# Reordering the last pass of a two-layer decode backward kernel: streamed chunks ahead of kept ones

## The chip, the cores and the metric

The kernel runs on one core of a Trainium2 chip. The metric is the device time of one launch in microseconds (us). A core has TensorE (PE, matrix multiplies), VectorE (DVE), ScalarE (ACT), GpSimd (POOL) and SyncE (SP); in this kernel SP only issues loads and POOL mostly issues stores. Both kinds of transfer run on the same 16 DMA engines.

## What is computed

The reference is a forward pass of two layers, used twice, and its vector-Jacobian product (`jax.vjp`). Shortened:

```
def A(x, k_cache, v_cache, wq, wo):      # B=2, one query, 32 heads, 4 kv heads, Sk=16384, Dh=128
    q = (x @ wq) per head;  k, v = caches repeated 8 times
    p = softmax(q k^T / sqrt(Dh));  return (p v) @ wo
def B(x, w1, b1, w2, b2):                # D=1024, F=3584
    return gelu(layernorm(x) @ w1 + b1) @ w2 + b2
x = x + A(layernorm(x)); x = x + B(layernorm(x))
x = x + A(layernorm(x)); x = x + B(layernorm(x))
outputs: x, and the gradients of x, k_cache, v_cache, wq, wo, w1, b1, w2, b2
```

Everything is bf16. Each cache is 32 MiB, so each of dK and dV is 32 MiB to store; the weight gradients are another 30 MiB.

## The kernel before, in words

The caches are cut into 8 groups `g` (batch times kv head) of 4 chunks (`NCH`) of 1 MiB each, 32 chunks (`NC`) per cache. A chunk is a tile of 128 partitions by 8 KB, one contiguous 8 KB run of memory per partition. The forward layers and the backward of the upper layer read the caches chunk by chunk. The last pass is the backward of the lower attention layer, and it also makes everything that is stored: dK and dV (the sum over both layers), dwq, dwo, dw1, dw2.

**The last pass** begins at line 1396 and has its main loop at L1438. Chunk indices `i` follow `order`: the first group's four chunks (i = 0 to 3) are *kept*, that is they still lie in tiles `keepV0..3` and `keepK0..3` from earlier; the 28 others are *streamed* (loaded again; chunk 4 of both caches was kept too, in `keepxV`, `keepxK`). A step `m` of the loop does, in this order: for two slots `k`, eight transposes of a V chunk and their copy out (`kT`, L1453), the score products of the slot before last (`score0`, L1317) and, at the end of a chunk, `ds0` (L1319), which makes dX, the score gradient, on DVE; a turn of one dwq operand (`late_pe`); one half of a *pair* each for K (k = 0) and V (k = 1); then the operand block of the next pairs (`make_blks`, four transposes per cache, L999); what `Sched` has due (`dq_quad`, which multiplies dX with the K chunk into dq); some units of weight gradients (`step_fill`); and new loads (`pump`).

**A pair** (`kv_pair`, L1247) is what makes a 1 MiB chunk of dK or dV, in two halves `h`: each has eight matmuls into four PSUM banks and four copies of 128x512 into half of a *home* tile, and stores that half (512 KB, 4 KB per partition). `v_at` and `k_at` (L1432) say in which step a chunk's first half comes. Before: V chunk i in step 2i - 3 (from i = 2), K chunk i one step after 2i - 4 for a streamed chunk, and after i - 1 for a kept one (K 31 one step sooner). So the kept K chunks take steps 0 to 3 and the two kept V chunks that are left steps 1 and 3; V 0 and 1 are made ahead of the loop.

**Fill.** A unit (`dw_units`, L1162) is one matmul of 4 rows into 128x512 and one copy; 4 or 8 units fill a part of a home tile, which is stored as two rows of 128 at a time. There are 240 such units, two for the biases, and nine units (`rows_unit`) that turn operands into rows. Before, `step_fill` takes one in each of steps 0 to 3 and five in every later step. The last 16 units (the last quarter of dwq) can only be made when dq of the last group is known.

**Tiles.** Loads, homes and fill share about 16 tiles of 1 MiB. A tile that has been read goes on the list `by_read`, one whose store has been issued on `by_store`; homes come from `by_read` first, loads from `by_store` first, oldest first. A load into a tile whose store has not landed waits on the SP queue, and the loads behind it with it; a copy into such a home waits on its engine. `pump` keeps at most 10 loads open in the first four steps and 7 later. The tile of `keepV0` holds dX of the kept chunks until the block of K chunk 3 is made.

**The end.** After the last chunk's dX: two `dq_quad`, the copy of the sums (`evac`), `reduce`, then `quarter` (L1293), which puts the 16 last units on `late` and three items on `tail`: the products with wq in two parts (L1282) and the layer norm backward (`last`); then the store of the x gradient.

Of the kernel before, what the change touches and what calls it, by code (L numbers as in the profile page):

```python
# [9 lines left out]
BF16 = mybir.dt.bfloat16  # L10
# [13 lines left out]
def kernel(  # L24
# [25 lines left out]
    V = nc.vector  # L50
# [15 lines left out]
    TC = 32  # L66
    NCH = T // TC
# [959 lines left out]
            V.tensor_copy(out=diag[:, t], in_=gcols.unsqueeze(1).to_broadcast([128, 4, n]))  # L1027

    def q_make(w, g, bank):
        Qm = wrk2.tile([128, 2, 128], BF16, name="Qm" + w)  # L1030
        for t in range(2):
            PE.matmul(bank[:, t * 128:(t + 1) * 128], lhsT=spr[w][:, t * 128:(t + 1) * 128], rhs=ident[:],
                      start=True, stop=True)
        evac_cast(Qm[:].rearrange("p a b -> p (a b)"), bank[:, 0:256], 256)
        qms[w, g] = Qm
# [101 lines left out]
    def store(out_ap, view, tile_):  # L1137
        nc.gpsimd.dma_start(out_ap, view)
        if tile_ is not None:
            by_store.append(tile_)  # L1140
# [21 lines left out]
    def dw_units(xrows, yrows, i, chunks, y0, ny, out_of):  # L1162

        ps_, tpos = (slice(0, 128), None) if i is None else (slice(32 * i, 32 * i + 4), (32 * i, 0))
        box = {}
        units = []
        for j0, rb in chunks:
            for j in range(rb):
                for c0 in range(0, ny, 512):
                    def u(j0=j0, rb=rb, j=j, c0=c0):  # L1170
                        if j == 0 and c0 == 0:
                            box["t"] = new_home()
                        sv_ = box["t"][:, 0:rb * ny].rearrange("p (j n) -> p j n", j=rb)
                        ps = mx()
                        PE.matmul(ps[:], lhsT=xrows[ps_, (j0 + j) * 128:(j0 + j + 1) * 128],  # L1175
                                  rhs=yrows[ps_, y0 + c0:y0 + c0 + 512], start=True, stop=True, tile_position=tpos)
                        evac_cast(sv_[:, j, c0:c0 + 512], ps[:], 512)
                        if c0 + 512 >= ny and (j % 2 == 1 or j == rb - 1):
                            js = j - j % 2
                            store(out_of(j0 + js, j + 1 - js), sv_[:, js:j + 1], box["t"] if j == rb - 1 else None)  # L1180
                    units.append(Unit(u, j == 0 and c0 == 0))
        return units

# [61 lines left out]
    stgs = {}  # L1245

    def kv_pair(w, i, h):  # L1247

        g, c = chunks[i]
        if h == 0:  # L1250
            stgs[w, i] = new_home()
        sv_ = stgs[w, i][:].rearrange("p (b r t d) -> p b r t d", r=4, t=2, d=128)
        blk, Qm = blks[w, i], qms[w, g]
        o = 0 if w == "V" else NB
        pss = [mx() for _ in range(4)]
        for b in range(2):
            for r in range(4):
                PE.matmul(pss[r][:, b * 256:(b + 1) * 256], lhsT=blk[32 * r:32 * r + 32, o + 2 * h + b, :],  # L1258
                          rhs=Qm[32 * r:32 * r + 32, :, :].rearrange("p a b -> p (a b)"), start=True, stop=True,
                          tile_position=(32 * r, 0))  # L1260
        for r in range(4):
            evac_cast(sv_[:, 2 * h:2 * h + 2, r], pss[r][:].rearrange("p (b t d) -> p b t d", b=2, t=2), 512)
        dst = (dVv if w == "V" else dKv)[g, :, c * TC + h * TC // 2:c * TC + (h + 1) * TC // 2, :]
        store(dst, stgs[w, i][:, h * LDW // 2:(h + 1) * LDW // 2].rearrange("p (t d) -> p t d", d=128),
              stgs[w, i] if h == 1 else None)

    dwq_v = out_4.rearrange("(j p) n -> p j n", p=128)
    quarters = {}
# [7 lines left out]
    def in_rows(q, kv):  # L1276
        box, ps = q[4], pm_([128, 512], F32, "dn_tail")

        def part(a):
            for j in range(a, a + 4):  # L1280
                for o in range(8):
                    PE.matmul(wide_out(ps, 2 * j), lhsT=box[j - j % 4][:, j % 4, o * 128:(o + 1) * 128],  # L1282
                              rhs=wide_in(dq_all[:, kv * 8 + o, 0:2]), start=(o == 0), stop=(o == 7))

        def last():
            V.tensor_tensor(out=dn0[:], in0=dn0[:], in1=pairs(ps, DJ), op=ALU.add)
            g0 = attn_in_bwd(0, g1, dn0, lambda: step_fill(1), lambda: step_fill(2))
            tail.append(lambda: col_to_row_f32(g0, DJ, out_1.rearrange("b s d -> (b s) d"), "o1",
                                               ktp.tile([128, 8, 128], BF16, name="o1", tag="kT")))

        return [lambda: part(0), lambda: part(4), last]

    def quarter(kv):  # L1293

# [45 lines left out]
    def dq_quad(i, q):  # L1340
        g, c = chunks[i]
        accs[g].coef = lambda u: dX[i][:, u - c * CP, 0].rearrange("p h t -> p (h t)")
        accs[g].quad(c, q)
        if q == 1:
            if g == G - 1:
                by_read.append(held_tiles["K%d" % c])
            else:
                done("K", g, c)

    def score0(s):  # L1350
        i, b = NCH + s // NB, s % NB
        g, c = chunks[i]
        if b == 0:
            dps["t"] = pm_([128, 16, TC], F32, "dp")
        scores(i, b, kTs.pop(s), dps["t"])
        if b < NB - 1:
            return
        if c == 0:
            open_dq(g)
        if order.index(g) % 2 == 1 and c == (2 if i < 2 * NCH else 0):  # L1360
            quarter_loads(g % HKV)
        ds0(i, dps["t"][:])
        end = 1 if i == NC - 1 else 2
        sch.later(1, lambda: dq_quad(i, 0))
        sch.later(end, lambda: dq_quad(i, 1))
        if c == NCH - 1:
            sch.later(end, accs[g].evac)
            sch.later(end + 1, accs[g].reduce)

    def step_fill(n):  # L1370
        for k in range(n):
            for q in ((late, fill) if k % 2 == 0 else (fill, late)):
                if q and q[0].ready():
                    q.popleft()()
                    break
# [53 lines left out]

    v_at = {2 * i - 3: i for i in range(2, NC)}  # L1432
    k_at = {(i - 1 if i < NCH else 2 * i - NCH - (i == NC - 1)): i for i in range(NC)}
    make_blks(None, 0)
    NS = (NC - NCH) * NB
    zero = {}
    m = 0
    while 2 * m < NS + 12 or late or fill or late_pe or tail or m <= max(v_at) + 2:  # L1438
        sch.s = m
        qs = []  # L1440
        iv, ik = v_at.get(m + 1), k_at.get(m)
        for w, i in (("V", iv), ("K", ik)):
            if i is not None and chunks[i][1] == 0 and (w, chunks[i][0]) not in qms:
                qs.append(make_qm(w, chunks[i][0]))
        for k in range(2):
            s = 2 * m + k
            if s < NS:
                i, b = NCH + s // NB, s % NB
                cv = get("V", *chunks[i])[:].rearrange("p (t d) -> p t d", d=128)
                kT = ktp.tile([128, 8, 128], BF16, name="kT", tag="kT")  # L1450
                tp = mtp()
                for j in range(8):
                    PE.transpose(tp[:, j, :], cv[:, b * 8 + j, :], ident[:])  # L1453
                evac_bf16(kT[:].rearrange("p a b -> p (a b)"), tp[:].rearrange("p a b -> p (a b)"), 1024)
                kTs[s] = kT
                if b == NB - 1:
                    done("V", *chunks[i])
                if b == 0 and chunks[i][1] == 0:
                    wg = chunks[i][0]
                    V.tensor_copy(out=wide_do[wg][:, :, 3], in_=cols["V"][:, wg].rearrange("p l r -> p (l r)"))  # L1460
            if 0 <= s - 2 < NS:
                score0(s - 2)
            if late_pe and (k == 1 or s >= NS or len(late_pe) > 6):
                late_pe.popleft()()
            at, w, m_ = ((k_at, "K", m - 1), (v_at, "V", m))[k]
            for h in range(2):
                if at.get(m_ - h) is not None:
                    kv_pair(w, at[m_ - h], h)
            if tail:
                tail.popleft()()  # L1470
        for f in qs:
            f()
        if iv is not None or ik is not None:
            make_blks(iv, ik)
        sch.run_slot(1)
        if m == NS // 2 - 8:
            zero["t"] = new_home()
            nc.gpsimd.memset(zero["t"][:, 0:2 * D], 0.0)
            nc.gpsimd.tensor_copy(out=zero["t"][96:100, 0:D], in_=rowsB[96:100, :])
        step_fill(1 if m < NCH else 5)  # L1480
        pump(NLD + 3 if m < NCH else NLD, 3)
        m += 1

# [29 lines left out]
```

## Time and profile before

| what | us |
|---|---|
| median of 7 runs | 1143.64 (1140.7 to 1147.08) |
| the profiled execution | 1142.9 |
| its span, first to last instruction | 1141.1 |
| PE busy | 938.1 (82%) |
| DVE busy | 633.0 (55%) |
| ACT busy | 564.8 (49%) |
| POOL busy | 117.8 (10%) |
| first kT transposes of step 0 of the last pass | at 743.13 |
| those of step 9 | at 797.11 |
| those of step 49 | at 1055.32 |
| those of step 50 | at 1073.31 |
| dX of the last chunk (step 56) | at 1104.63 |

The profile has a page with busy times, the span in 40 slices, DMA queues (q1 carries the loads of SP, q0 the stores of POOL), the chain that ended last, and groups of instructions. Further views are tables by stage, the timeline of an engine or a queue, and waits. The DMA share of a stage is the mean busy share of the 16 DMA engines (it can read a little over 1), GB/s is what they moved.

### The profile page before, as it was taken

The numbers are of one execution on the slowest core, as the hardware profiler recorded it, in microseconds if no ns is written. First come the engines' busy times: TensorE is split into PE (matmuls) and PEld (weight loads), VectorE is DVE, ScalarE is ACT, GpSimd is POOL, SyncE is SP. The second block draws the span as 40 slices with busy tenths as digits, with TensorE's granted clock in tenths as the row PEclk, the third lists the DMA queues.
The fourth block names the chain that finished last, engine by engine and source line by source line (L and its number), as shares of the span: only waits on it lengthen the run. The fifth ranks groups of instructions, "written<-read, shape, count | busy, mean of one in ns | idle before, by whom it ended". The sixth has DMA issues, their size and how long they took to land. (4 is left out here: it accounts for less than half of the span.)

```text
span 1141.1 us, 40256 instructions
## 1 busy us (share of the span) xinstructions
PE 938.1 (82%) x17565; PEld 725.4 (64%) x17567; DVE 633.0 (55%) x1357; ACT 564.8 (49%) x1415; POOL 117.8 (10%) x206
## 2 busy tenths in 40 slices
PE   4988896487879885899997799989888888998585
PEld 3867674387767765888775588855555554554352
DVE  1535442133544433544845355678887876887385
ACT  0534351022535430344554354667777866867373
POOL 0000000000000000000000000022232222222323
PEclk9989785587998976899998799998988987987796
DMA  9999999998999989999999999998999999999997
GB/s 370 424 424 424 425 424 413 409 362 352 423 426 420 425 327 423 402 360 406 375 421 420 348 368 356 346 376 307 415 421 420 419 415 413 371 407 409 411 400 293
DMA packets 98717, 449.33 MB, mean 394 GB/s; under 512 B 8418, under 2 KB 8418, under 8 KB 67564
## 3 DMA queue, kind: packets, MB, share of 16 engines
q1 hardware_dynamic: 72204, 348.17, 76.1%
q0 software_dynamic: 26336, 98.60, 21.3%
q8 instruction: 137, 2.24, 0.7%
q14 instruction: 40, 0.33, 0.1%
HBM read 348.14 MB, written 98.58 MB: 391 GB/s over the span
## 5 line engine op out<-in xcount | busy, mean ns | idle before, releaser
L153 ACT COPY kT<-tp 128x512 int32<-128x512 int32 x209 | 122.8, 588 | 253.9 <-PE tp L420 243.0
L156 DVE COPY kT<-tp 128x1024 bf16<-128x1024 bf16 x159 | 108.7, 691 | 108.7 <-PE tp L420 96.9
L420 PE MATMUL tp<-ident,kv_K 128*128 128x128 bf16 x1728 | 142.9, 231 | 4.3 <-DMA kv_K<-in_A_k_cache_dram 4.0
L420 PEld LDWEIGHTS <-kv_K 128*128 128x128 bf16 x1728 | 108.6, 103 | 5.2 <-DMA kv_K<-in_A_k_cache_dram 4.5
L164 DVE CAST big<-xm 128x512 bf16<-128x512 f32 (+1 forms) x125 | 81.1, 685 | 36.3 <-DMA out_dram<-big 16.3
L161 ACT CAST big<-xm 128x512 bf16<-128x512 f32 (+1 forms) x139 | 75.7, 593 | 38.9 <-DMA out_dram<-big 17.6
L573 PEld LDWEIGHTS <-kT 128*128 128x128 bf16 x2048 | 76.3, 98 | 27.4 <-issue 21.2
L573 PE MATMUL sc<-qT_bf,kT 128*128 128x8 bf16 x2048 | 92.0, 171 | 0.2
L420 PE MATMUL tp<-ident,kv_V 128*128 128x128 bf16 x864 | 69.3, 226 | 11.6 <-DMA kv_V<-in_A_v_cache_dram 10.7
L270 PE MATMUL wtp<-ident,wt 128*128 128x128 bf16 x928 | 75.3, 228 | 3.8 <-issue 2.6
L537 ACT ACTIVATE e_all<-sc,negm 128x64 bf16<-128x64 f32 x256 | 77.2, 345 | 1.2 <-DVE negm L532 1.1
L306 PEld LDWEIGHTS <-wt 128*128 128x128 bf16 x1696 | 49.1, 104 | 43.9 <-issue 15.4
L161 ACT CAST keepV<-xm 128x512 bf16<-128x512 f32 x118 | 64.6, 595 | 23.0 <-PE xm L1258 17.2
L452 PE MATMUL acc_all<-kv_V,e_all 128*16 128x256 bf16 x864 | 46.2, 294 | 26.8 <-DMA kv_V<-in_A_v_cache_dram 13.9
L156 DVE COPY wT<-wtp 128x1024 bf16<-128x1024 bf16 (+1 forms) x64 | 40.7, 641 | 49.2 <-PE wtp L270 45.6
L153 ACT COPY wT<-wtp 128x512 int32<-128x512 int32 (+1 forms) x60 | 34.3, 572 | 64.1 <-PE wtp L270 49.9
L164 DVE CAST keepV<-xm 128x512 bf16<-128x512 f32 x86 | 55.7, 685 | 18.0 <-PE xm L1258 7.1
L164 DVE CAST keepK<-xm 128x512 bf16<-128x512 f32 (+1 forms) x87 | 56.5, 685 | 13.8 <-PE xm L1258 6.8
L420 PEld LDWEIGHTS <-kv_V 128*128 128x128 bf16 x864 | 54.7, 101 | 13.5 <-DMA kv_V<-in_A_v_cache_dram 11.4
L161 ACT CAST keepK<-xm 128x512 bf16<-128x512 f32 (+1 forms) x95 | 51.7, 592 | 19.3 <-PE xm L1258 12.0
L270 PEld LDWEIGHTS <-wt 128*128 128x128 bf16 x928 | 57.8, 102 | 4.5 <-issue 3.1
L537 ACT ACTIVATION_READ_ACCUMULATOR e_all<-sc,negm 128x1 f32 x256 | 60.1, 235 | 0.0
(368 smaller groups left out, 1823.8 us busy)
## 6 DMA issues: line engine op xcount, KB each, us to landing
kv_K<-in_A_k_cache_dram SPq DMA_DIRECT2D x81, 1024.0 KB, 12.2
kv_V<-in_A_v_cache_dram SPq DMA_DIRECT2D x81, 1024.0 KB, 12.1
wt<-in_A_wo_dram SPq DMA_DIRECT2D x32, 1024.0 KB, 10.9
out_dram<-big POOLq DMA_DIRECT2D x62, 512.0 KB, 15.6
wt<-in_B_w_dram SPq DMA_DIRECT2D x32, 896.0 KB, 14.1
out_dram<-keepV POOLq DMA_DIRECT2D x44, 512.0 KB, 14.1
out_dram<-keepK POOLq DMA_DIRECT2D x42, 512.0 KB, 15.4
wt<-in_A_wq_dram SPq DMA_DIRECT2D x16, 1024.0 KB, 9.2
```

Of the source, the lines that this page charges most:

```text
L153: S.copy(out=dst.bitcast(I32), in_=src.bitcast(I32))
L156: V.tensor_copy(out=dst, in_=src)
L161: S.copy(out=dst, in_=src)
L164: V.tensor_copy(out=dst, in_=src)
L270: PE.transpose(tp[:, o, :], wv[:, j, (o0 + o) * 128:(o0 + o + 1) * 128], ident[:])
L306: PE.matmul(fps[:, jo, :].rearrange("p (a b) -> p a b", b=2), lhsT=wv[:, j, jo * 128:(jo + 1) * 128], rhs=xT_bf[:, j0 + j, :].unsqueeze(1) ...
L420: PE.transpose(tp[:, j, :], cv[:, b * 8 + j, :], ident[:])
L452: PE.matmul(self.acc[cg:cg + 16, :], lhsT=coef(u), rhs=self.cv[:, t:t + 2, :].rearrange("p t d -> p (t d)"), start=False, stop=True, tile_ ...
L537: S.activation(out=e_all[:, g, f * half:(f + 1) * half, l, h, :], in_=sc[g][f][:, h, :].rearrange("p (a b) -> p a b", b=2), func=ACT.Exp, ...
L573: PE.matmul(sc[g][f][:, :, t % TH], lhsT=kT[:, j, :], rhs=q_bf[:, g, :], start=True, stop=True)
```

## The change

It touches only the last pass.

- The order: streamed V chunk i has its pair in step 2i - 7 (four steps sooner), streamed K chunk i has its block made in step 2i - 6 and its pair one step later (two steps sooner, K 31 one). The kept K chunks come in between, with blocks made in steps 9, 15, 21, 27, kept V 2 and 3 in steps 20 and 28. The block of K 0 is no longer made ahead of the loop. The first group's Q tiles get homes of their own, since they are needed until step 29.
- Fill: steps 4 to 8 take one `rows_unit` each, steps 0 to 8 no other unit, and five a step come from step 9.
- Stores: a pair of chunks 2 to 29 is stored whole (1 MiB, 8 KB per partition) instead of by halves; a dW tile is stored whole too.
- The end: each slot takes two `tail` items, one ahead of the pair halves and one behind them, where it took only the one behind. The last chunk's two `dq_quad` and `evac` become a `tail` item and so come straight behind its dX, ahead of the pair half of that slot; `reduce`, the next item, comes behind that half. The two parts of the wq product are one item, and an empty item follows it.

```diff
@@ q_make
-        Qm = wrk2.tile([128, 2, 128], BF16, name="Qm" + w)
+        Qm = (vec if g == g0_ else wrk2).tile([128, 2, 128], BF16, name=("Q0" if g == g0_ else "Qm") + w)
@@ dw_units
-                        if c0 + 512 >= ny and (j % 2 == 1 or j == rb - 1):
-                            js = j - j % 2
-                            store(out_of(j0 + js, j + 1 - js), sv_[:, js:j + 1], box["t"] if j == rb - 1 else None)
+                        if j == rb - 1 and c0 + 512 >= ny:
+                            store(out_of(j0, rb), sv_, box["t"])
@@ kv_pair
-        dst = (dVv if w == "V" else dKv)[g, :, c * TC + h * TC // 2:c * TC + (h + 1) * TC // 2, :]
-        store(dst, stgs[w, i][:, h * LDW // 2:(h + 1) * LDW // 2].rearrange("p (t d) -> p t d", d=128),
-              stgs[w, i] if h == 1 else None)
+        n = TC if 2 <= i < NC - 2 else TC // 2
+        if h == 1 or n < TC:
+            t0 = h * n if n < TC else 0
+            dst = (dVv if w == "V" else dKv)[g, :, c * TC + t0:c * TC + t0 + n, :]
+            store(dst, stgs[w, i][:].rearrange("p (t d) -> p t d", d=128)[:, t0:t0 + n], stgs[w, i] if h == 1 else None)
@@ in_rows
-        return [lambda: part(0), lambda: part(4), last]
+        return [lambda: (part(0), part(4)), lambda: None, last]
@@ score0
-        end = 1 if i == NC - 1 else 2
+        if i == NC - 1:
+            tail.append(lambda: (dq_quad(i, 0), dq_quad(i, 1), accs[g].evac()))
+            tail.append(accs[g].reduce)
+            return
         sch.later(1, lambda: dq_quad(i, 0))
-        sch.later(end, lambda: dq_quad(i, 1))
+        sch.later(2 if i < NC - 2 else 1, lambda: dq_quad(i, 1))
         if c == NCH - 1:
-            sch.later(end, accs[g].evac)
-            sch.later(end + 1, accs[g].reduce)
+            sch.later(2, accs[g].evac)
+            sch.later(3, accs[g].reduce)
@@ the loop
-    v_at = {2 * i - 3: i for i in range(2, NC)}
-    k_at = {(i - 1 if i < NCH else 2 * i - NCH - (i == NC - 1)): i for i in range(NC)}
-    make_blks(None, 0)
+    v_at = {2 * i - 7: i for i in range(NCH, NC)}
+    k_at = {2 * i - NCH - 2: i for i in range(NCH, NC)}
+    for i in range(NCH):
+        k_at[9 + 6 * i] = i
+    for i in range(2, NCH):
+        v_at[4 + 8 * i] = i
...
             if late_pe and (k == 1 or s >= NS or len(late_pe) > 6):
                 late_pe.popleft()()
+            if tail:
+                tail.popleft()()
             at, w, m_ = ((k_at, "K", m - 1), (v_at, "V", m))[k]
...
-        step_fill(1 if m < NCH else 5)
+        if NCH <= m < 2 * NCH + 1:
+            fill.popleft()()
+        step_fill(0 if m < 2 * NCH + 1 else 5)
```

## The prediction

> **What bounds the kernel now.** I read the slices of the page first, then a table by stage of the last pass, then the load queue, and last the chain that ended last. The page, DMA share and GB/s in 40 slices of 28.5 us:
>
> ```profile
> DMA  9999999998999989999999999998999999999997
> GB/s 370 424 424 424 425 424 413 409 362 352 423 426 420 425 327 423 402 360 406 375 421 420 348 368 356 346 376 307 415 421 420 419 415 413 371 407 409 411 400 293
> ```
>
> The DMA engines are busy nearly always, so what has to be moved bounds the kernel, and only stretches below the usual rate can be won. The last pass starts at slice 27 (307). By stage (columns: window, length, busy time and count of PE, PEld, DVE, ACT, POOL, granted PE clock, DMA share, GB/s):
>
> ```profile
> 742.00:755.00 13.00, 10.53 (x172) 8.43 (x176) 9.12 (x21) 7.48 (x16) 2.47 (x5) 0.87 1.01 413
> 755.00:795.00 40.00, 35.96 (x530) 23.25 (x529) 32.56 (x57) 30.89 (x61) 9.71 (x19) 0.91 0.88 310
> 795.00:960.00 165.00, 142.58 (x1922) 85.15 (x1918) 129.42 (x229) 121.56 (x234) 43.83 (x75) 0.87 1.02 418
> 960.00:990.00 30.00, 28.09 (x368) 17.98 (x367) 24.75 (x45) 22.92 (x45) 8.78 (x15) 0.85 0.98 364
> 1080.00:1090.00 10.00, 8.17 (x149) 6.13 (x142) 8.65 (x19) 7.86 (x17) 4.69 (x7) 1.00 1.00 352
> 1120.00:1141.00 21.00, 10.87 (x111) 4.55 (x110) 11.10 (x25) 7.71 (x15) 5.64 (x9) 0.66 0.63 256
> ```
>
> 418 GB/s over 165 us is what this mix of loads and stores reaches when the queues are full. Measured by it, a stage loses its length times (1 - rate/418): 755 to 795 loses 10.3 us, 960 to 990 3.9, 1080 to 1090 1.6, the end 8.1, the rest (413 from 990 to 1080, 412 from 1090 to 1120, 413 at first) 1.7. Together **25.6 us**, the most that any order of the same bytes could win here. Compute is close behind: steps 8 to 20 (five units, two pair halves each) start from 791.73 to 865.45, 6.14 us each, while one step asks for 2.625 MiB = 2.75 MB, 6.6 us at 418.
>
> Why 755 to 795 is thin shows on SP's queue (start, length, load):
>
> ```profile
> 758.80 0.33 SPq L1207 DMA_DIRECT2D keepK<-in_A_k_cache_dram  x1
> 775.19 0.33 SPq L1207 DMA_DIRECT2D big<-in_A_v_cache_dram  x1
> 786.28 0.33 SPq L1207 DMA_DIRECT2D keepxV<-in_A_k_cache_dram  x1
> 796.04 0.33 SPq L1207 DMA_DIRECT2D keepV<-in_A_v_cache_dram  x1
> ```
>
> Three loads start in 36 us; later it is one per step. The tiles lie as homes of kept pairs. And the end, from the chain in order of time (start, length, what):
>
> ```profile
> 1104.63 0.68 DVE dX L1325
> ...
> 1109.42 0.96 PE acc_all L452 x12
> ...
> 1116.54 0.26 DVE dq_all L904 x2
> ...
> 1118.83 0.59 PE xm L1175
> ...
> 1135.13 0.76 POOLq L1508
> ```
>
> From the last dX to the end of the span are 36.5 us, with compute in single file and DMA idle 37% of the last 21.
>
> **The opening, steps 0 to 8.** Before they take 743.13 to 797.11, 54 us. After, steps 0 to 8 lose 8 halves of kept K and 4 of kept V and gain 6 of streamed chunks, and no dW unit runs until step 9. Steps 50 to 55 of before are of that kind (no units, two pair halves): 1073.31 to 1101.83, 4.75 us each over six. A half is four copies of 0.59 to 0.69 us on two engines, 1.3 us. So step 0 (no half) costs 4.75 - 2.6 = 2.2, steps 1 and 2 (one) 3.4 each, steps 3 to 8 4.75 each: 37.5 us, and step 9 starts near 781. That alone wins nothing, the work comes later; what counts is whether DMA is fed. On offer until 781: about 3.4 MB of loads and 0.8 of stores that are under way at 742 (the load queue moved 3.65 MB from 740 to 760, 0.3 of it of a load issued at 758.8); two loads whose tiles are those of V 0 and 1, stored before the loop, so free by about 750 instead of 758.8 and 775.2; three loads as the stores of V 5, 6, 7 land; and seven chunks stored, 7.3 MB. With 5.2 MB of loads that is 16.8 MB, and DMA could move 39 x 0.418 = 16.3. Just enough; but stores come only at the end of even steps, in pairs of 1 MiB, so gaps remain. Ends: loss gone (wins 10.3) or as before (wins 0). I take the middle, **5 us**.
>
> **The middle.** The same bytes; the six kept chunks (12 halves, 1.3 us each) raise both compute and DMA demand of steps 9 to 29. Three things cost. (a) The K block is now transposed in the step whose dX it reads: PE waits for 0.69 us of DVE work, behind the V half (0.4 to 1.2 us of matmuls) that lies between. 28 times 0 to 0.7 is 0 to 20 us of PE; hidden by the 0.46 us a step that DMA is slower than compute. If that cover is gone, as where stores hold a home up, it costs up to 0.7 a chunk. Queued behind the waiting transposes are the `dq_quad`, the units and the next kT. (b) Followed through the code, the lists give a load a tile mostly two steps after its store was issued (three before), since one tile less is around until step 27 and homes take more. (c) Stores wait for a whole chunk; POOL issues 103 instead of 182 of them at 0.53 to 0.72 us, and it is busy a quarter of the time, so nothing is won or lost there; a store behind one that waits is of a later half anyway. I take the two dips (5.5 us) as staying, **0**; ends: they go (-5.5), or they come twice more (+11).
>
> **Whole-chunk stores.** 56 MiB of pairs (58.7 MB) go from 4 KB to 8 KB runs. No row shows an 8 KB store. Stores alone (1110 to 1120) moved 407 GB/s, loads of 8 KB runs alone (slices 1 to 5) 424: were it all the run, 58.7/0.407 - 58.7/0.424 = 5.8 us would go. Stores with 7 KB runs lie inside the 418 stage and hurt nothing there, so below 0 only the 1% between 418 and 413 is left: 1.7 us lost. The mixed stage is nearest to after, 418 against 424, a third of the gap: **1 us** won, doubtful. [...]
>
> **The end.** After, `dq_quad` follows dX at once. From dX to the ready dq: dX 0.68, quads 0.97, copy 0.42, `reduce` behind one half (1.0 + 1.2), scaling and cast 0.44: about 4.7 instead of 12.2 (1116.8). The first of the last units comes 7.4 us sooner. From there to the last store's issue before are 16.3 us with three pair halves in it; two now: 15. The last store is 1 MiB, not 512 KB: 0.52 MB / 0.407 = +1.3. So dX to the end: 36.5 - 7.4 - 1.3 + 1.3 = 29 us. It is worth less than 7.5, since DMA must still move what is queued at that dX plus 3.5 MiB (V half, two K halves, 2 MiB of dwq). At a backlog of 4 to 8 MB that is 18 to 28 us of DMA, so 1 to 11 us idle; at 6 MB 29 - 23 = 6 against 8.1: **2 us** won; ends -3 and +7. dX itself comes sooner by what the opening and middle win.
>
> **Sum.** 5 + 0 + 1 + 2 = 8 us off the profiled execution, 1142.9 to 1134.9; the median lies 0.74 above that execution, so 1135.6.
>
> **Rivals.**
> - *Tiles starve (slower).* Loads arrive late in steps 11 to 35, PE waits in order for V, and DMA falls into turns of stores, then loads. Speaks for it: at 948 to 960 and 1056 to 1073 kT already stood still, one copy waiting 12 us for a store, and losses of 3.9 and 1.6 us followed, 2.75 each; (a) to (c) above make such stalls likelier. Against: while a copy waits for a store, DMA is by that very fact busy. Eight more stalls cost 22 us against 8 won: 1143.6 + 14 = 1157.6. It decides from the third extra stall (2.75 x 3 > 8). Chance 0.21.
> - *It only moves the gaps.* The opening now has stores in even steps only, a gap each, and the end's backlog is small: wins 0 to 2, 1143. Chance 0.13.
> - *Both ends fill and the rate rises.* 10 of the opening, 5 of the end, 3 of the stores: 18 won, 1126. Chance 0.18.
>
> **How the numbers follow.** The forecast, 3 to 13 us won (1131 to 1141), has 0.48. With the third rival, faster is 0.66; within 0.2% (2.3 us, about what a measurement can tell here) 0.13; slower 0.21. The range leaves out the lower third of the third rival and the upper half of the first: 1124 to 1151.
>
> **What would show it.** Right: loads starting near 745 to 750 and every 4 to 9 us after; over 360 GB/s for the 40 us after 755; step 9 near 781; the last dX before 1100, dq 5 us behind it, the end 29 behind. Wrong: PE waiting for a block's transposes on dX's DVE work by more than 0.9 us a chunk; copies waiting for stores more than six times; a rate under 410 in steps 9 to 49 (rival one); the same 8 us idle at the end with the opening at 310 (rival two).

## The result, and the profile after

The changed kernel is **slower**: median 1152.93 us (1146.49 to 1159.4, 13 runs) against 1143.36 us (34 runs of the kernel before), ratio 1.0082 with the interval 1.0064 to 1.0101. The prediction had 1135.6 us and a range up to 1151: direction and range were both wrong. The profiled execution took 1151.35 us, its span is 1149.6 (before 1142.9 and 1141.1).

The page of the changed kernel: TensorE's granted clock, DMA share and GB/s by slice, and the chain that ended last.

```profile
PEclk9988895597989975899998899998858868967786
DMA  9999999998999989999999899998999999999994
GB/s 371 424 424 425 423 424 412 408 361 366 425 424 423 423 319 423 392 372 405 383 419 420 307 356 354 370 354 324 378 414 394 421 388 415 420 416 418 424 421 196
...
PE 19%; DVE 3%; ACT 3%; issue 1%; DMA 1%; POOLq 0%; DVEq 0%; ACTq 0%
```

The last slice fell from 293 to 196 GB/s: DMA runs dry at the end. PE has 19% of the chain that ended last, which can be followed back to 829 us; before, it could be followed only to 1102 us, and PE had 2%. By stage (window, length, busy time and count of PE, PEld, DVE, ACT, POOL, clock, DMA share, GB/s):

```profile
755.00:795.00 40.00, 36.56 (x637) 26.07 (x635) 32.07 (x58) 30.52 (x60) 4.78 (x9) 0.96 0.86 315
795.00:825.00 30.00, 26.84 (x360) 17.02 (x360) 21.22 (x37) 19.43 (x38) 4.21 (x7) 0.77 0.97 365
825.00:920.00 95.00, 82.01 (x982) 48.55 (x979) 73.23 (x127) 69.14 (x134) 14.25 (x25) 0.78 1.01 410
920.00:960.00 40.00, 34.83 (x405) 19.69 (x406) 27.68 (x49) 25.65 (x49) 4.75 (x8) 0.66 1.00 392
960.00:1120.00 160.00, 144.76 (x1817) 89.26 (x1817) 124.77 (x215) 117.20 (x223) 30.03 (x48) 0.80 1.02 420
1120.00:1149.60 29.60, 14.24 (x144) 6.66 (x138) 12.45 (x29) 9.07 (x17) 3.99 (x7) 0.62 0.50 202
```

Against 418 GB/s the opening loses 9.9 us (10.3 before) and 3.8 more behind it, 825 to 960 some 4.3, the end 15.3 (8.1 before). The loads of the opening do start sooner, yet the gap has only moved to where the next stores are awaited:

```profile
747.98 0.33 SPq L1206 DMA_DIRECT2D keepV<-in_A_k_cache_dram  x1
755.55 0.33 SPq L1206 DMA_DIRECT2D keepV<-in_A_v_cache_dram  x1
769.38 0.33 SPq L1206 DMA_DIRECT2D big<-in_A_k_cache_dram  x1
780.74 0.33 SPq L1206 DMA_DIRECT2D big<-in_A_v_cache_dram  x1
```

The end, from the chain in order of time:

```profile
1119.24 0.61 DVE dX L1326
1119.89 0.61 PE acc_all L452 x16
...
1122.73 0.63 PE tpm L1101 x8
...
1124.20 1.01 PE xm L1175 x2
...
1142.87 0.79 POOLq L1519
```

Behind the last dX all goes as meant: dq's turn starts 3.5 us after dX, and 30.4 us of span are left (36.5 before). But this dX comes at 1119.2 instead of 1104.6. Step 9 starts at 780.83 (before 797.11), 16 us sooner, and steps 9 to 55 then take 336 us, 7.15 each, where they took 304.7, 6.48 each. These 31 us are more than the opening and the end (6 us) give back. All of them lie in steps 9 to 30, which now make the kept chunks. From the first transposes of step 9 to those of step 31, and from there to those of step 49, first the kernel before, then the changed one:

```profile
797.11:937.21 140.10, 123.21 (x1705) 76.25 (x1704) 111.64 (x200) 104.24 (x200) 37.73 (x66) 0.88 1.02 418
937.21:1055.32 118.11, 104.63 (x1339) 60.71 (x1338) 93.06 (x163) 87.32 (x167) 31.54 (x53) 0.84 1.01 400
```

```profile
780.83:954.12 173.29, 150.29 (x1821) 89.37 (x1822) 127.85 (x220) 119.89 (x229) 25.04 (x44) 0.75 0.99 388
954.12:1072.55 118.43, 106.18 (x1340) 64.02 (x1340) 93.16 (x163) 88.17 (x169) 19.00 (x32) 0.81 1.02 418
```

Steps 9 to 30 take 33 us more, steps 31 to 48 the same 118 us. The same pass cut at the last dX, first the kernel before, then the changed one:

```profile
742.00:1104.63 362.63, 310.33 (x4275) 192.15 (x4276) 277.56 (x493) 259.32 (x497) 97.34 (x163) 0.86 1.00 399
1104.63:1141.10 36.47, 22.04 (x210) 10.19 (x211) 20.47 (x44) 16.17 (x30) 12.03 (x21) 0.65 0.79 319
```

```profile
742.00:1119.15 377.15, 335.70 (x4355) 209.69 (x4355) 287.70 (x504) 269.64 (x514) 59.40 (x99) 0.80 0.99 399
1119.15:1149.60 30.45, 14.35 (x144) 6.77 (x146) 13.14 (x31) 9.07 (x17) 4.20 (x7) 0.63 0.51 208
```

Two readings fit the last four lines. **Bytes:** both kernels move 399 GB/s up to the last dX, 144.7 MB and 150.5 MB; the 5.8 MB more, stores put ahead of the last loads, are 14.5 us at that rate, just the delay of the last dX. **TensorE:** PE does some 4,490 matmuls in either pass (4,485 and 4,499 records), but is busy 350.1 us instead of 332.4 and idle 57.5 instead of 66.7. So 9.2 us of its waiting did go, and the same matmuls took 17.7 us longer. The experiments decide between the two.

### The profile page after: what moved, and what is told of

Read it like the earlier page. It is cut to its first block, busy times and chain, and to the rows that moved or that the text cites. A ratio compares the mean times of both kernels' runs of the same rounds, so it can differ in the third digit from the quotient of the medians.

```text
span 1149.6 us, 40003 instructions
## 1 busy us (share of the span) xinstructions
PE 953.0 (83%) x17565; PEld 738.5 (64%) x17567; DVE 635.3 (55%) x1355; ACT 567.4 (49%) x1418; POOL 71.5 (6%) x127
## 5 line engine op out<-in xcount | busy, mean ns | idle before, releaser
L161 ACT CAST big<-xm 128x512 bf16<-128x512 f32 (+1 forms) x150 | 81.1, 593 | 22.3 <-PE xm L1257 16.8
L164 DVE CAST big<-xm 128x512 bf16<-128x512 f32 (+1 forms) x117 | 76.2, 686 | 20.5 <-PE xm L1257 13.7
L164 DVE CAST keepV<-xm 128x512 bf16<-128x512 f32 x93 | 60.8, 686 | 22.8 <-PE xm L1257 14.8
L161 ACT CAST keepV<-xm 128x512 bf16<-128x512 f32 x114 | 61.3, 593 | 23.3 <-PE xm L1257 19.5
L452 PE MATMUL acc_all<-kv_V,e_all 128*16 128x256 bf16 x864 | 46.0, 293 | 29.1 <-DMA kv_V<-in_A_v_cache_dram 15.3
L161 ACT CAST keepK<-xm 128x512 bf16<-128x512 f32 x106 | 57.0, 591 | 19.9 <-PE xm L1257 16.0
L164 DVE CAST keepK<-xm 128x512 bf16<-128x512 f32 x84 | 54.5, 686 | 14.1 <-PE xm L1257 9.1
```

What stands on the lines that cost most here:

```text
L161: S.copy(out=dst, in_=src)
L164: V.tensor_copy(out=dst, in_=src)
L452: PE.matmul(self.acc[cg:cg + 16, :], lhsT=coef(u), rhs=self.cv[:, t:t + 2, :].rearrange("p t d -> p (t d)"), start=False, stop=True, tile_ ...
```

## The experiments

Each kernel is compared with the kernel before on the same chip; where two edited kernels are compared, it is by these ratios. "Before with" and "after with" tell which kernel was edited. Times of steps and stages come from the one profiled execution of each kernel.

### Which part of the change costs

**Before with the end part alone** (the hunks `in_rows` and `score0`, and the `tail` item ahead of the pair halves):

```diff
+            tail.append(lambda: (dq_quad(i, 0), dq_quad(i, 1), accs[g].evac()))
+            tail.append(accs[g].reduce)
```

> The kernel before with the end part alone (last dq ahead of the pair half, two tail items a slot, the wq products as one item); order, fill and stores as before. Theory P (from step 9 on PE is the bound, at a clock that falls as it is packed; the end part is sound by itself): dq is ready 5 to 8 us after the last dX instead of 12.2, the end 31 to 34 us after it instead of 36.5, dX itself where it was (1104 +- 4), ratio to before 0.996 to 0.999. Theory S (the loss is in the whole-chunk stores) and theory D (in the fill put off) say the same of this run. If the end part itself did the harm, ratio over 1.003.

Measured 1.0019 (1.0001 to 1.0037), so the gain was missed. The last dX is at 1105.6 and dq follows at once, but the pair halves that are still to come wait behind it, and from 1120 on they run at half clock. The end is 39.2 us long, not 31 to 34:

```profile
1120.00:1144.80 24.80, 13.95 (x72) 4.48 (x69) 11.71 (x19) 10.41 (x20) 6.54 (x11) 0.50 0.58 233
```

**Before with whole-chunk stores alone** (the hunks `dw_units` and `kv_pair`):

```diff
+                            store(out_of(j0, rb), sv_, box["t"])
```

> The kernel before with the stores alone (whole chunks of 1 MiB for pairs 2 to 29 and whole dW tiles). Theory S: stores come later and in lumps, loads wait for whole tiles, so a large share of the +0.8% appears here: ratio 1.004 to 1.010, rate in steps 9 to 49 under 410. Theory P: DMA is not what waits, ratio 0.998 to 1.003, and the granted clock from 780 to 1120 stays at 0.84 to 0.86.

Measured 0.9988 (0.9964 to 1.0013): no harm (theory S falls). The middle of the interval, 1.4 us won by 79 fewer and larger stores together, is close to the 1 us that the prediction gave them. The clock from 780 to 1120 is 0.83, a little under what theory P had.

**Before with the order alone** (`v_at`, `k_at`, the Q tiles):

```diff
+    v_at = {2 * i - 7: i for i in range(NCH, NC)}
+    k_at = {2 * i - NCH - 2: i for i in range(NCH, NC)}
```

> The kernel before with the order of the pairs alone (streamed first, kept ones spread, Q tiles of their own); fill from step 0 and 4 as before, stores by halves, end as before. Theory P: PE gets the streamed pairs sooner and the kept ones in the middle, the DMA stalls of before vanish and the clock falls to 0.77 to 0.82; the last dX is later by 5 to 12 us, ratio 1.002 to 1.008. Theory D: the order alone is harmless, 0.996 to 1.001. Theory S the same as D.

Measured 1.0112 (1.0076 to 1.0148). The order carries all of the harm, and a little more than the whole change. Theory P had the sign; the last dX at 1124.3, 19.7 us later, and the clock from 780 to 1100, 0.75, are further off than it said.

**After with the fill of before** (units from the first steps on):

```diff
-        if NCH <= m < 2 * NCH + 1:
-            fill.popleft()()
-        step_fill(0 if m < 2 * NCH + 1 else 5)
+        step_fill(1 if m < NCH else 5)
```

> The changed kernel with only the fill schedule put back (one unit in steps 0 to 3, five from step 4). Theory D: the 24 units that were put off were the harm; the stretch 795 to 825 recovers from 365 to over 400 GB/s, the last dX comes 6 to 10 us sooner, ratio to before 0.996 to 1.001. Theory P: PE has the same work in all, only earlier; the opening is slower by what the middle wins, ratio 1.004 to 1.010. Theory S as P.

Measured 1.0088 (1.0054 to 1.0122): the units that the change holds back are not the cause (theory D falls).

Then the order in pieces. **Before with the kept K chunks spread alone:**

```diff
+    k_at = {2 * i - NCH - (i == NC - 1): i for i in range(NCH, NC)}
+    for i in range(NCH):
+        k_at[9 + 6 * i] = i
```

> The kernel before with the kept K chunks alone moved to steps 9, 15, 21, 27 (Q tiles of their own); streamed pairs, kept V, fill, stores and end as before. If the harm of the order lies in spreading the kept chunks into steps that are full already (theory C: three or four pair halves of 32 rows in one step starve the array): ratio 1.003 to 1.010, clock 780 to 960 at 0.73 to 0.80. If it lies in taking the streamed pairs sooner: 0.998 to 1.002, clock as before (0.87).

**Before with the streamed K pairs one step sooner alone:**

```diff
-    k_at = {(i - 1 if i < NCH else 2 * i - NCH - (i == NC - 1)): i for i in range(NC)}
+    k_at = {(i - 1 if i < NCH else 2 * i - NCH - 1): i for i in range(NC)}
```

> The kernel before with the streamed K pairs alone one step sooner (block one step behind the chunk's dX instead of two), all else as before, kept chunks first. If taking streamed pairs sooner does the harm, PE waiting for dX with its transposes: ratio 1.003 to 1.010. If the spreading of the kept chunks does it: 0.997 to 1.002, the last pair halves one step earlier.

**Before with the new order of V alone:**

```diff
-    v_at = {2 * i - 3: i for i in range(2, NC)}
+    v_at = {2 * i - 7: i for i in range(NCH, NC)}
+    for i in range(2, NCH):
+        v_at[4 + 8 * i] = i
```

> The kernel before with the new order of V alone: streamed V pairs four steps sooner, kept V 2 and 3 at steps 20 and 28, Q tiles of the first group of their own; K as before. The whole order costs 1.12%, the kept K chunks spread alone 0.30%, streamed K one step sooner alone nothing. If the parts add up, V carries the rest: ratio 1.005 to 1.010, last dX between 1112 and 1120. If it is only the sum of both that empties a reserve, V alone stays at 0.998 to 1.003.

Measured 1.0030 (1.0005 to 1.0055), 0.9993 (0.9968 to 1.0018) and 1.0076 (1.0047 to 1.0105). They sum to 0.99%, against 1.12% for the whole order: V, with streamed pairs four steps sooner and the kept V 2 and 3 in steps 20 and 28, carries two thirds of it, the kept K chunks most of the rest. They are not quite its parts, since the change takes streamed K two steps sooner and the run one.

### Bytes or TensorE

**After, and before, with two more transposes behind each unit** (a load on TensorE that nothing reads):

```diff
+    def warm(n):
+        tp = TP[rot["tp"] % 2]
+        for j in range(n):
+            PE.transpose(tp[:, j, :], ident[:], ident[:])
...
                     q.popleft()()
+                    warm(2)
```

> The changed kernel with two extra transposes of the identity (full 128x128 array, results overwritten unread) behind every fill unit: more PE work, 2 x 0.055 us at full clock a unit, about 27 us in all if PE ran at 1.00 throughout. Theory C (PE is the bound, and its clock falls to half when the array gets little full-width work for some microseconds, as between the 4-row matmuls of the fill and the 32-row ones of the pairs): the half-clock time of 153 us in the last pass falls under 80, the mean clock from 780 to 1120 rises from 0.78 to over 0.88, and the kernel gets faster in spite of the work: ratio to before 0.985 to 1.003. Theory W (PE is bound by its amount of work, the clock falls for another reason): the extra work comes on top, ratio 1.015 to 1.035.

> The kernel before with the same two extra transposes behind every fill unit. Theory C: half-clock time falls from 111 us, clock 780 to 1120 from 0.85 to over 0.90; DMA is then the bound from step 4 on, ratio 0.985 to 1.000. Theory W: 1.005 to 1.025.

Measured 1.0766 (1.0738 to 1.0794) and 1.0423 (1.0389 to 1.0457), some 79 and 49 us. As a cure for the clock they failed (theory C as it stood then falls: the clock from 780 to 1120 is 0.72, where the changed kernel has 0.78). As a probe they tell that work on TensorE alone is paid for in both, and that the kernel before hid 30 us more of it.

**After, and before, without the products of the units** (the copies and stores stay):

```diff
-                        PE.matmul(ps[:], lhsT=xrows[ps_, (j0 + j) * 128:(j0 + j + 1) * 128],
-                                  rhs=yrows[ps_, y0 + c0:y0 + c0 + 512], start=True, stop=True, tile_position=tpos)
```

> The changed kernel with the 4-row matmul of every weight-gradient unit left out (some 240 in the last pass and the 16 late ones; dW1, dW2, dwq and dwo are then whatever lies in the bank, the copies and stores stay as they are). It is the opposite of the dummies. Theory P (TensorE sets the pace of the changed kernel from step 9 on, at 7.15 us a step): a unit's price with two dummies added was 0.33 us, the unit alone has one narrow matmul in that, so five units a step are some 0.5 to 1.6 us a step; over 47 steps 25 us or more go until DMA binds at 6.6 us a step, so the time falls to 1115 to 1130, ratio to the kernel before 0.975 to 0.99, with DMA from 780 to 1100 at 415 GB/s or more. Rival Q (the order hurts by when tiles come free or by how reads and writes mix, TensorE only follows): the time stays within 0.5% of the changed kernel's, ratio 1.003 to 1.013.

> The kernel before with the 4-row matmul of every weight-gradient unit left out in the same way. Theory P: it had DMA losses of 25.6 us in all, of which 10.3 lie at 755 to 795 and 8.1 in the end, where TensorE matters little, so it can win less than the changed kernel: ratio 0.985 to 0.997. Rival Q: no change, 0.997 to 1.003. If it gains as much as the changed kernel does, TensorE bound both alike and does not tell them apart.

Measured 0.9957 (0.9930 to 0.9984) and 0.9981 (0.9959 to 1.0004). The changed kernel wins 1.25% by it, the kernel before 0.2%. The first is less than expected. The changed kernel without the products, steps 9 to 30 and 31 to 48:

```profile
779.33:938.68 159.35, 128.66 (x1714) 83.26 (x1714) 124.12 (x219) 115.29 (x227) 24.50 (x43) 0.78 0.99 399
938.68:1058.76 120.08, 94.60 (x1257) 63.09 (x1253) 91.78 (x164) 84.76 (x168) 18.39 (x31) 0.76 1.02 422
```

Steps 9 to 30 are 14 us shorter. Steps 31 to 48 are not shorter, with 12 us less of PE work and a lower clock, at 422 GB/s: TensorE does not set the pace there, and the rate is that of full queues (418 before).

**After, and before, with 6.3 MB less stored** (all products and copies stay):

```diff
+            if w == "V" and 8 <= i < 20:
+                n = TC // 2
+                dst = dst[:, 0:n]
```

> The changed kernel, which stores only the first half of the V chunks 8 to 19 (12 times 512 KB, 6.3 MB of dV are left out; all products and copies stay). Theory L (the last loads wait for the bytes stored ahead of them): 6.3 MB at 399 GB/s are 15.8 us, so the last dX comes at 1102 to 1106 (1119.15) and the time falls by as much, ratio to the kernel before 0.991 to 0.998. Theory P (TensorE sets the pace): the steps go on at 7.1 us, last dX 1115 to 1120, ratio 1.004 to 1.010.

> The kernel before, with the first halves of the V chunks 8 to 19 not stored (the same 6.3 MB left out). Theory L: last dX sooner by 15.8 us at 1088 to 1092, ratio 0.983 to 0.990. Theory P says that DMA bound the kernel before as well, at 6.48 us a step, but that its compute was close behind: it gains a part, 0.988 to 0.996. With both runs: if the two kernels fall by the same, bytes are what counts in both.

Measured 1.0088 (1.0055 to 1.0121) and 0.9943 (0.9911 to 0.9975). This fells the reading by bytes for the stretch in which they are missing. With 6.3 MB gone, the changed kernel's last dX is no sooner and its DMA rate falls instead, while the kernel before gets there 8.9 us sooner. The changed kernel, then the one before, each with less stored:

```profile
742.00:1122.09 380.09, 336.77 (x4337) 208.82 (x4337) 286.96 (x504) 269.14 (x513) 58.76 (x98) 0.78 0.96 380
```

```profile
742.00:1095.71 353.71, 317.07 (x4306) 199.29 (x4306) 279.54 (x495) 261.45 (x500) 92.56 (x154) 0.85 0.99 395
```

The chunks in question have their pairs in steps 9 to 32 of the changed kernel. With less stored, its steps 9 to 30 and 31 to 48 are:

```profile
777.92:957.02 179.10, 154.97 (x1822) 92.07 (x1822) 128.04 (x220) 120.24 (x229) 24.93 (x44) 0.71 0.92 348
957.02:1076.55 119.53, 106.51 (x1340) 63.66 (x1340) 93.42 (x163) 88.31 (x169) 20.10 (x32) 0.81 1.02 417
```

That 5.8 MB happened to be 14.5 us at 399 GB/s was a coincidence of sizes. In steps 9 to 30 of the changed kernel TensorE sets the pace and bytes do not, and a DMA share of 0.99 at 388 GB/s proves nothing: stores follow at the pace at which they are made. From step 31 on it is the other way round as far as the runs tell, though none of them takes bytes away there. One rival is left for steps 9 to 30: PE also waits there for copies on ACT and DVE, some 21 us in pieces of at most 0.8 us, and no run takes copies away.

### Where the last pairs stand

**After with the pairs of chunks 28 to 31 where the kernel before has them** (below), **and half way** (5 in place of the 3, and 1 for K):

```diff
+    v_at = {2 * i - (7 if i < 28 else 3): i for i in range(NCH, NC)}
+    k_at = {2 * i - NCH - (2 if i < 28 else i == NC - 1): i for i in range(NCH, NC)}
```

> The changed kernel with the pairs of the last four chunks of V and K (28 to 31) in the steps where the kernel before has them; all else, the kept chunks spread and the streamed pairs up to chunk 27 sooner, stays. Theory L: the bytes ahead of the last dX go back to some 145 MB, so it comes at 1103 to 1109; the end after it is again some 36 to 39 us long, ratio 0.998 to 1.004. Theory P: the steps up to 50 are those of the changed kernel, so the last dX gains at most what six pair halves cost on TensorE, some 1.5 us each: it stays at 1110 or later, ratio 1.004 to 1.012.

> The changed kernel with the pairs of chunks 28 to 31 put back half way (V two steps later, K one). Theory L: 147 to 148 MB ahead of the last dX, which comes at 1109 to 1114, 9 MB behind it, an end of 30 to 34 us, ratio 1.000 to 1.006. Theory P: as for the pairs put back whole, 1.004 to 1.010.

Measured 1.0090 (1.0058 to 1.0122) and 1.0089 (1.0060 to 1.0119). With the six halves back, the last dX is 6.2 us sooner, about 1 us per half, and the end after it 9.2 us longer. Moving these pairs across the last dX wins nothing here.

### What makes the same matmuls slower

Mean times of most groups rise together, those of the scores by 5% and those of the K pairs by 8%, while the products of the units rise by only 1 to 3% (400 and 403 ns to 404 and 414). The scores and the K pairs, the kernel before first (line, engine, shapes, count, busy us, mean ns):

```profile
L1317 PE MATMUL dp<-wdo,kT 128*128 128x64 bf16 x896 | 53.6, 207 | 0.0
...
L1258 PE MATMUL xm<-QmK,blk 32*128 32x256 bf16 x480 | 30.6, 305 | 3.3 <-DVE keepV L164 1.9 <-ACT keepV L161 0.7 <-DVE blk L156 0.3
```

```profile
L1318 PE MATMUL dp<-wdo,kT 128*128 128x64 bf16 x896 | 57.9, 217 | 0.0
...
L1257 PE MATMUL xm<-QmK,blk 32*128 32x256 bf16 x432 | 30.5, 330 | 3.5 <-ACT big L161 1.3 <-DVE keepV L164 1.0 <-ACT keepxK L161 0.7
```

At a fine grain the granted clock of both profiles has two values, 1.00 and 0.50, here called full and half (68 stretches in the kernel before, 92 in the changed one), and every stretch but the last, which the end of the profile cuts off, lasts 3.41 us or a multiple of it. The changed kernel in such windows:

```profile
809.59:813.00 3.41, 3.07 (x38) 1.41 (x36) 3.06 (x6) 2.67 (x6) 0.86 (x2) 1.00 1.03 395
813.01:816.42 3.41, 3.41 (x90) 2.88 (x90) 2.52 (x5) 2.53 (x5) 0.72 (x2) 1.00 1.02 420
816.42:819.83 3.41, 3.11 (x49) 1.50 (x46) 2.42 (x5) 2.28 (x5) 0.06 (x1) 1.00 1.00 387
819.83:823.24 3.41, 3.41 (x43) 2.40 (x44) 2.15 (x5) 2.06 (x4) 1.54 (x3) 0.50 1.01 377
823.25:826.66 3.41, 3.23 (x45) 1.54 (x37) 3.14 (x5) 3.03 (x6) 1.03 (x2) 1.00 0.96 340
...
850.55:853.96 3.41, 3.41 (x42) 2.64 (x41) 2.56 (x5) 1.56 (x3) 0.73 (x2) 0.50 1.05 393
853.97:857.38 3.41, 2.23 (x35) 1.22 (x34) 2.76 (x5) 2.66 (x7) 0.86 (x2) 1.00 1.00 374
857.38:860.79 3.41, 3.29 (x33) 2.19 (x32) 1.49 (x3) 1.57 (x4) 0.76 (x1) 0.50 1.03 432
...
867.62:871.03 3.41, 2.27 (x40) 1.45 (x37) 3.03 (x6) 2.89 (x7) 0.53 (x1) 1.00 1.07 435
```

PE's busy time does not tell what comes next: 3.11 us (816.42) is followed by a window at half clock, 2.27 (867.62) by one at full clock. The *array work* of a window does better: the sum over its matmuls of rows x weight columns x moved columns, over 128 x 128. Eight transposes count 1024, a pair half 512, four dq products 128, a unit's product 4/128 x 512 = 16. A matmul that lies across the edge of a window is shared out by its time; since some records are missing, the sums are good to a few per cent. By the timeline of PE the windows above have

| window | array work | the next window's clock |
|---|---|---|
| 809.59 | 3140 | full |
| 813.01 | 5040 | full |
| 816.42 | 1910 | half |
| 819.83 | 3770 | full |
| 850.55 | 3830 | full |
| 853.97 | 2590 | half |
| 857.38 | 3050 | full |
| 867.62 | 3650 | full |

Over the 2142 windows of the last pass in 18 profiles of this case, with a bound at 2860 fitted to them, the next window is full at or above it and half below it in 94 of 100 (93 in the kernel before, 97 in the changed one). Other measures of a window, each with the bound that suits it best, do worse: the number of matmuls 88, the moved columns 72, the busy time 70. Up to the last dX the mean is 3190 in the kernel before and 3120 in the changed one, close to the bound; 26% and 38% of the windows lie below it, and 72% and 59% run at full clock. The difference is made in steps 9 to 30, where the mean falls from 3240 to 2780, under the bound.

**After, and before with whole-chunk stores, with more of the array in use** by the same matmuls: dq products with 32 weight columns (16 more, whose sums are left out), unit products with 32 rows (28 of them zero).

```diff
-        ps_, tpos = (slice(0, 128), None) if i is None else (slice(32 * i, 32 * i + 4), (32 * i, 0))
+        ps_, tpos = (slice(0, 128), None) if i is None else (slice(32 * i, 32 * i + 32), (32 * i, 0))
-        accs[g].coef = lambda u: dX[i][:, u - c * CP, 0].rearrange("p h t -> p (h t)")
+        accs[g].coef = lambda u: dX[i][:, u - c * CP].rearrange("p l h t -> p (l h t)")
```

> The changed kernel with the same matmuls and moved columns, but more of the array in use: the 16 dq products of a step take 32 weight columns in place of 16 (the 16 more give rows that the sum leaves out), and the products of the units take 32 rows in place of 4 (28 of them zero in one operand). That adds 16 x 16/128 x 256 = 512 and 5 x 28/128 x 512 = 560 column equivalents a step, some 515 per 3.41 us, to a mean of 3148. Theory G (the clock of a window goes by the array work of the one before it, with a bound near 2860): the clock between 742 us and the last dX rises from 0.80 to 0.88 or more, the last dX comes at 1100 to 1110, ratio to the kernel before 0.990 to 1.001. Rival (the clock goes by something else: how many matmuls or columns run, idle time, or the values themselves, so that rows of zeros count nothing): clock 0.78 to 0.82, ratio 1.006 to 1.010.

> The kernel before with whole-chunk stores (alone 0.9988) and the same fuller products. Theory G: the clock between 742 us and the last dX rises from 0.86 to 0.91 or more, and the end, where the pairs run at half clock, stays as it is; DMA bound this kernel in part (6.3 MB fewer gave 0.57%, no unit products 0.2%), so little is left to gain: ratio 0.990 to 0.998. Rival: 0.996 to 1.002, with the clock at 0.84 to 0.87.

Measured 1.0044 (1.0020 to 1.0069) and 0.9990 (0.9971 to 1.0009). The clock rises in both, though less than expected (0.84 for 0.88 in the changed kernel, 0.89 for 0.91 in the other), and the first time lies between the ranges of the two theories, the second in the rival's:

```profile
742.00:1115.28 373.28, 327.07 (x4375) 203.88 (x4371) 288.40 (x508) 269.69 (x514) 59.08 (x98) 0.84 0.99 399
```

```profile
742.00:1103.99 361.99, 305.42 (x4329) 189.32 (x4322) 279.04 (x497) 261.06 (x502) 56.23 (x93) 0.89 0.99 404
```

The same bound of 2860, found before them, tells 94 of 100 windows right in these two profiles; mean work up to the last dX is 3520 and 3590. Over all runs, the clock of the whole span is 0.852 before (102 runs), 0.837 after (14), 0.853 after with the fuller array (12); it is 0.850 before with whole-chunk stores (11) and 0.866 with the fuller array as well (12). From one run of the changed kernel to the next, 0.01 of clock goes with 5.5 us of time (correlation -0.91), in the kernel before with 3.3; which of the two drives the other this does not tell, since the same work in a longer pass is also less work per window. Against the changed kernel the fuller array wins 0.38%, give or take 0.31 (the two intervals' halves added in squares): about half of the loss, with the clock of the span back at that of the kernel before. It reaches its last dX 3.9 us sooner and still 10.7 us later than the kernel before does. Where the time was lost, in steps 9 to 30, it changes little: 171.0 us at a clock of 0.78 against 173.3 at 0.75, with 43% of the windows still below the bound; from step 31 on its clock is 0.87 instead of 0.81, but there DMA has the pace (117.3 us at 421 GB/s). The other version only matches the kernel before, since there the clock was not what was short; no version that does all of the work beats it by more than a measurement can tell.

**Before with whole-chunk stores and the three weight gradients in turn:**

```diff
+            dw_units(rowsB, rowsA, 1, list(w_chunks(D, F)), 0, F, rows_of(out_6)),
+            dw_units(rowsA, rowsB, 2, list(w_chunks(HD, D)), 0, D, rows_of(out_5))]
```

> The kernel before with whole-chunk stores (alone 0.9988) and the units of the three weight gradients taken in turn (dW2, dW1, dwo) instead of dW2 and dW1 in turn and then dwo, so that neighbouring 4-row matmuls come from different row groups of TensorE in all of the pass. Theory P: what shortens the units on TensorE shortens the pass a little where dwo units stood in a row: ratio 0.990 to 0.998. Rival: three open tiles in place of two hold a tile of 1 MiB more and loads come later, or the price of a unit does not depend on its neighbour: 0.998 to 1.006.

Measured 1.0110 (1.0075 to 1.0144), as the rival had it and worse. The rate of the opening falls: 309 and 346 GB/s, where the kernel before with whole-chunk stores alone has 335 and 391 in these windows. That fits a third open tile as one tile less for loads; it was not tested apart from the order of the units.

```profile
742.00:780.00 38.00, 32.82 (x465) 24.38 (x466) 26.36 (x52) 23.60 (x47) 4.78 (x9) 0.82 0.77 309
780.00:860.00 80.00, 72.07 (x944) 44.60 (x944) 61.67 (x107) 58.67 (x111) 11.30 (x19) 0.81 0.86 346
```

## Why the prediction was wrong

- **What bounds.** "Compute is close behind", 6.14 us a step against 6.6, was true of the kernel before, where taking away bytes helps (0.57%) and taking away products hardly does (0.2%). It was carried over to the changed kernel as a cover, and in steps 9 to 30 that cover is gone. This is the step that failed: "the middle, **0**", and with it "dX itself comes sooner by what the opening and middle win". The middle cost TensorE time: the last dX is 14.5 us later.
- **What the middle should have cost.** The working had some of the pieces. Steps 9 to 30 take over the 12 halves of the kept chunks. At the prediction's own 1.3 us a half, which it took from the copies and not from TensorE, these are 15.6 us on top of the 140.1 that the steps took before, 155.7 in all, just what the opening gives back (16.3). The other 17.6 us up to the measured 173.3 are what nobody priced: 6.14 us a step was read at a clock of 0.87, and these steps now run at 0.75, where they had 0.88. An estimate from these rows: 155.7 x 0.88 / 0.75 = 183 if all of it were TensorE at that clock; 173.3 lies between. One reason fits: a half counts 512 of array work, which at 1.3 us a half is 1340 in 3.41 us, less than half of the bound, so these halves thin out the windows that they are put into. From step 31 on nothing is lost (118.4 against 118.1).
- **The opening.** Right in its mechanism (step 9 at 780.83, forecast 781; loads at 748 and 755.6), wrong in its worth: 315 GB/s from 755 to 795 where over 360 was asked for, a loss of 9.9 + 3.8 us for 10.3. The sum had 5 us won; the doubt stated there, stores only in even steps with gaps between, was right: up to 800 us the load queue waits three times for stores from `big`, up to 13.4 us.
- **Stores.** 1 us forecast; alone they lie between 4 us won and 1.5 lost, so the term is neither confirmed nor refuted.
- **The end.** 29 us forecast, 30.4 measured, dq 3.5 us behind dX for 4.7. The backlog was mis-sized: 6.33 MB are moved in the whole end, of which 3.7 were still to be made, so 2.7 MB waited at the last dX, not 4 to 8, and DMA loses 15 us there, not 6.
- **Waits.** (a) cost nothing: PE waits 0.2 us in all for dX's DVE work at the transposes. The wait for a store that stood in front of a pair half is gone, as was meant. Before (us, times, longest):

```profile
PE xm L1258 <- ACT big L161: 13.4, 3, 12.0
```

After, no wait of PE up to the last dX is longer than 1.3 us, and these are the largest sums:

```profile
PE xm L1032 <- ACT big L161: 3.5, 5, 0.8
PE xm L1032 <- ACT keepK L161: 2.6, 4, 0.7
```

- **The rivals.** *Tiles starve* had the right sign and, by luck, nearly the size (1157.6), but not the cause: its mark, a rate under 410, came (372 GB/s from 780 to 860), but up to the last dX no copy waits for a store and no matmul for a load. An engine that becomes the bound was a rival that the list lacked.

**What stays open.** That TensorE sets the changed kernel's pace in steps 9 to 30 is shown by the runs without products and with less stored, and the one with dummies agrees. That its clock fell there is measured; how much of the 17.6 us the clock took is not. The fuller array wins 1 to 8 us (0.38% give or take 0.31) of 9.5, but lifts the clock of these steps only from 0.75 to 0.78. Against the clock as the whole cause: the kernel before with streamed K one step sooner has 0.79 from 780 to 1100 (0.85 without the edit) and loses no time. Nor do the runs tell what each of the two, kept pairs put in and waits taken out, does to the array work. A hint of the second: waits come in lumps before (the 12 us one), which leaves a few windows very low and the rest high (tenth percentile 1460, quarter 2830), while without them the work is even and below or near the bound (1960 and 2350).

## What to carry to other kernels

A DMA share near 1 does not say that bytes set the pace (0.99 in steps 9 to 30 here, and 6.3 MB less stored brought the last dX no sooner): leave some bytes out, and some work of the next engine, and see which moves the end. Do this stage by stage, since one pass can have two bounds, as steps 9 to 30 and 31 to 48 have here. Before shifting work into a stretch, redo that stretch's sum for every engine with the work in it, at the clock that it will have. A stall that is taken away is worth little where the engine behind it has no room (here 9.2 us of PE's waiting went, and its matmuls took 17.7 us longer), and work that moves ahead of a late event can delay it (about 1 us of the last dX per pair half here).

## What the runs showed of the hardware

- The granted clock read 1.00 or 0.50, in stretches of 3.41 us or a multiple of it (two profiles). In 94 of 100 windows of 18 profiles, and of two more, it was full after a window with an array work of 2860 or more and half after one with less. That is a bound fitted to this kernel's runs, not shown for another mix of matmuls. With rows of zeros and columns that no one reads added, the clock of the span rose from 0.837 to 0.853; which of the two did it was not shown.
- A unit's product counts 16 of array work at a mean of 400 ns, a transpose 128 at 230 to 258 (kernel before). Two full-width transposes behind each unit did not help: they cost 0.33 us a unit in the changed kernel, and the clock up to the last dX was 0.74 against 0.80.
- 79 fewer stores on POOL's queue, each up to 1 MiB instead of 512 KB, changed the time by less than 0.4%, though POOL's busy time in the profile fell from 117.8 to 71.5 us with the whole change.
